# Statistics per pair of heads, another order at the start, and six low-rank products one by one, in a fused attention and MLP kernel

## The chip, the cores and the metric

One core of one Trainium2 chip. The metric is device time in microseconds (us) for one execution, and I quote medians. PE is TensorE, DVE is VectorE, ACT is ScalarE, POOL is GpSimd, SP is SyncE.

## The reference

Cosine attention over 8 batches of 12 heads, 448 tokens and head size 64, then a low-rank token mixer and an MLP. Cut to what matters:

```python
q_n = q / (np.linalg.norm(q, axis=-1, keepdims=True) + 1e-06)
k_n = k / (np.linalg.norm(k, axis=-1, keepdims=True) + 1e-06)
attn = softmax(q_n @ k_n.T / tau)                  # [8, 12, 448, 448]
x = (attn @ v)                                      # heads side by side: [8, 448, 768]
u = x + ((x^T @ U) @ V)^T                           # rank 32 over the tokens
out = u + np.maximum(u @ w_ch1, 0.0) @ w_ch2        # 768 -> 3072 -> 768
```

## The kernel before

Every instruction is an `Op` with an engine, an estimated duration, dependencies, buffers that it takes (`acq`) and gives back (`rel`), and a priority. A planner, `Plan.run`, plays all of them through with the estimated durations, decides each engine's order, and emits them in that order. The program then makes each engine work **strictly in that order** and wait on semaphores. The planner's choice on an engine that isn't PE:

```python
                        for i, (_, _, o) in enumerate(w):
                            if o.start is not None:
                                continue
                            if e == "ACT" and o.fast and free["DVE"] <= t + 1e-9:
                                continue
                            r = self.ready_at(o, e)
                            if r is None:
                                continue
                            if r <= t + 1e-9:
                                pick = o
                                break
                            heapq.heappush(events, r)
                            if r <= t + self.HOLD:
                                break
                        if pick is not None:
                            del w[i]
# ... (cut)
```

The statistics of a group of heads: squares, sums over the 64 elements, then a logarithm and exponential (for the root), an addition, a reciprocal, and the product that normalises q and k:

```python
    def squares(b, g, ld, ops, lo, ii, ss, pr, on, hold):

        red = []
        for i in ii:
            for a0 in range(0, g, G // 2):
                a1 = min(g, a0 + G // 2)
                sq = Slot(r_sq, 1)
                o = Op(on, 0.48 if on == "ACT" else 0.44, None,
                       deps=[ops[i], *hold], acq=[sq], prio=pr + 0.2, fast=True)
                # ... (cut: the square itself, on ACT or DVE)
                red.append(plan.add(Op("DVE", dve_t(256 * (a1 - a0)),
                    lambda i=i, a0=a0, a1=a1, sq=sq: nc.vector.reduce_sum(
                    # ... (cut)
                    deps=[o], acq=[ss], rel=[sq], prio=pr + 0.1)))
        return red
    # ... (cut: scales = squares, then Ln, Exp, addition, reciprocal)
    def stats(b, h0, h1, ld, ops, lo, hold=()):

        pr = 0.3 + 0.03 * h0 if b == 0 else 4
        inv = Slot(r_inv, h1 - h0)
        o, _ = scales(b, h0, h1, ld, ops, lo, (0, 1), inv, pr, "DVE" if b else "ACT/DVE", hold)
        for p in range(h0 // 2, h1 // 2):
            o_ = norm(b, p, ld, lo + 2 * p - h0, inv, 2 * p - h0, {0: o, 1: o}, pr)
        return o_

    def stats_first(ld, ops):

        inv = Slot(r_inv, 3)
        done, ups = {}, []
        for i in range(2):
            done[i], up = scales(0, 0, 2, ld, ops, 0, (i,), inv, -1 - 0.1 * i, ("DVE", "ACT")[i])
            ups.append(up)
        return ups + norm(0, 0, ld, 0, inv, 0, done, -1)
```

In the attention of one pair of heads, seven blocks of scores go to ACT for the exponential and the result lands in one of two `attn` buffers, which the 32 products with v read:

```python
    attn_t = fixed(2, [128, 8, 512], BF, "attn")
    # ... (cut)
        attn = Slot(r_attn, 2)
        # ... (cut: seven scores and exponentials)
                    o = plan.add(Op("PE", 0.033, fn,
                        deps=need + got[b, h, "v"] + attn_set + [v_set[b % 2]] if first else (), acq=[av] if first else [],
                        rel=[attn] if last else []), pe_av)
```

The low-rank products of batch 0, six of them, go as one block in front of the tenth group of up-projections. Each takes one of three PSUM banks `mm`, which the up-projections use too:

```python
    def by_tokens(us, A, X):

        for i in range(3):
            for c0, c1 in ((0, CH), (CH, C)):
                mm = Slot(r_mm, 1)
                o = plan.add(Op("PE", pe_t(CH), lambda i=i, c0=c0, c1=c1, mm=mm: nc.tensor.matmul(
                    out=mm.tile[:, 0:CH], lhsT=V_sb[:, PAD + 128 * i:PAD + 128 * i + 128],
                    rhs=A.tile[:, c0:c1], start=True, stop=True), acq=[mm, us[i]], rel=[A]), pe_mlp)
                # ... (cut: an addition on DVE, which frees the bank)
    # ... (cut)
            if b == 0 and f == 9:
                by_tokens(us, *state["first"])
```

And the order of the start:

```python
    first = lead, [plan.add(Op("SP", 0.45, lambda i=i, src=src: nc.sync.dma_start(
        out=lead.tile[:, i], in_=src[0, 0:2].rearrange("h (s c) d -> s h (c d)", c=SC)),
        acq=[uv], prio=-5, lat=2.5)) for i, src in enumerate((q, k))]
    second = load_qk(0, 2, 4, uses=2)
    ld, ops, _ = load_qk(0, 4, 8)
    id_set = plan.add(Op("POOL", 0.8, lambda: make_identity(nc, ident)), pool_q)
    begun = stats_first(*first[:2])
    stats(0, 2, 4, *second, hold=begun)
    xn_set.append(fill(lambda: nc.vector.memset(xn_t[2][:, 0:8, :], 0.0), 900, prio=0.2, deps=begun))
    zf = fill(lambda: nc.vector.memset(U_f(), 0.0), 400, prio=0.1, acq=[uv], deps=begun)
    u0 = load_u(0)
    v0 = [plan.add(Op("SP", 0.45, lambda t=t: nc.sync.dma_start(out=V_f()[R * t:R * (t + 1)], in_=moe_V),
                      deps=[zf, *begun], prio=-2, lat=12.0)) for t in range(4)]
    u1 = load_u(1)
    stats(0, 4, 8, ld, ops, 0, hold=got[0, 0, "qkT"][2])
    load_v0()
    ld, ops, _ = load_qk(0, 8, 12)
    late = stats(0, 8, 12, ld, ops, 0)
```

## Time and profile before

| | before |
|---|---|
| median of 3 runs | 605.15 us (604.89 to 605.44) |
| span of the profiled run | 603.2 us |
| PE busy / DVE / ACT / POOL | 97% / 50% / 46% / 19% |
| last exponential of batch 0 starts | 37.3 us |
| first unbroken run of up-projections | 41.3 us |

The busy shares say that PE is the bound. They hide the two places where PE is not: the 41 us before the MLP begins, and a hole at 50 us. The prediction below shows the lines for both. For the comparison of stages I use **lost time**: from the trace, the time from the start of one of PE's weight loads to the start of the next, less what the matmul between them needs to stream at full rate (384 columns 0.163 us, 448 columns 0.19 us and so on). It does not depend on the modelled ends of matmuls, nor on some 23 matmul records that are missing from the trace of after.

### The profile page before, as it was taken

The numbers are of one execution on the slowest core, as the hardware profiler recorded it, in microseconds if no ns is written. First come the engines' busy times: TensorE is split into PE (matmuls) and PEld (weight loads), VectorE is DVE, ScalarE is ACT, GpSimd is POOL, SyncE is SP. The second block draws the span as 40 slices with busy tenths as digits, with TensorE's granted clock in tenths as the row PEclk, the third lists the DMA queues.
The fourth block names the chain that finished last, engine by engine and source line by source line (L and its number), as shares of the span: only waits on it lengthen the run. The fifth ranks groups of instructions, "written<-read, shape, count | busy, mean of one in ns | idle before, by whom it ended". The sixth has DMA issues, their size and how long they took to land.

```text
span 603.2 us, 11528 instructions
## 1 busy us (share of the span) xinstructions
PE 586.4 (97%) x4725; PEld 347.0 (58%) x4725; DVE 300.6 (50%) x728; ACT 276.9 (46%) x598; POOL 115.2 (19%) x175
## 2 busy tenths in 40 slices
PE   3899999999999999999999999999999999999997
PEld 1565666555565665666445666566545666654565
DVE  8979749989999988554731244014300210110011
ACT  5877652488874277316741067505642025014300
POOL 8246334062706116000600000000000000000000
PEclk9999999999999999999999999999999999999999
DMA  9999999999999959725922133030002110310021
GB/s 144 193 188 112 204 201 107 150 173 136 159 152 155 149 102 154 95 57 90 123 29 66 52 74 47 1 93 27 15 1 53 52 40 1 90 42 1 0 53 54
DMA packets 150165, 54.81 MB, mean 91 GB/s; under 512 B 115040, under 2 KB 150112, under 8 KB 150112
## 3 DMA queue, kind: packets, MB, share of 16 engines
q0 software_dynamic: 72864, 25.73, 38.4%
q1 hardware_dynamic: 77184, 28.32, 24.4%
q8 instruction: 37, 0.61, 0.4%
q14 instruction: 16, 0.13, 0.1%
q10 hardware_dynamic: 64, 0.02, 0.0%
HBM read 52.25 MB, written 11.01 MB: 105 GB/s over the span
## 4 chain that ended last, share of the span: by engine, by line
PE 93%; DVE 2%; ACT 2%; POOL 1%; DMA 1%; issue 0%; ACTq 0%; POOLq 0%
PE mm L794 36%; PE mm L760 35%; PE sc L572 10%; PE av L592 8%; PE mm L684 1%; PE tp L374 1%; DMA v_nat<-in_v_dram 1%; DVE xn L536 1%; PE mm L649 1%; POOL v_nat L429 1%; ACT attn L577 1%; PE sc L760 0%; POOL qk_nat L396 0%; DVE ss L461 0%; ACT qkT L824 0%
## 5 line engine op out<-in xcount | busy, mean ns | idle before, releaser
L760 PE MATMUL mm<-uT,w_sb 128*128 128x512 bf16 (+1 forms) x1134 | 241.3, 353 | 0.2 <-DVE u_nat L734 0.2
L794 PE MATMUL mm<-w_sb,relu 128*128 128x384 bf16 (+1 forms) x1368 | 231.3, 323 | 0.0
L577 ACT ACTIVATE attn<-sc 128x448 bf16<-128x448 f32 x336 | 164.6, 552 | 110.9 <-PE av L592 58.2
L794 PEld LDWEIGHTS <-relu 128*128 128x128 bf16 x1368 | 132.7, 98 | 86.1 <-issue 0.2
L760 PEld LDWEIGHTS <-w_sb 128*128 128x128 bf16 x1152 | 111.8, 98 | 102.7 <-issue 1.8
L783 ACT ACTIVATE relu<-mm 128x512 bf16<-128x512 f32 (+1 forms) x158 | 86.8, 549 | 129.3 <-PE mm L760 128.7
L803 DVE TENSOR_TENSOR O_sb<-mm,u_nat 128x384 f32<-128x384 f32 (+1 forms) x57 | 31.2, 549 | 210.8 <-PE mm L794 207.4
L572 PE MATMUL sc<-qkT 128*128 128x448 bf16 x336 | 102.7, 356 | 3.7 <-ACT attn L577 2.0
L592 PEld LDWEIGHTS <-attn 128*128 128x128 bf16 x1536 | 62.1, 98 | 17.8 <-issue 2.5
L418 POOL DMA_DIRECT2D v_nat<-in_v_dram x98 | 63.2, 655 | 31.7 <-DMA w_sb<-in_moe_w_ch_dram 15.8
L592 PE MATMUL av<-v_nat,attn 128*128 128x65 bf16 x1536 | 66.6, 194 | 0.8 <-DMA v_nat<-in_v_dram 0.4
L461 DVE TENSOR_REDUCE ss<-sq 112x8 f32<-112x512 bf16 x96 | 63.1, 673 | 0.2
L536 DVE TENSOR_TENSOR xn<-qk_nat,inv 112x512 bf16<-112x512 bf16 x94 | 60.9, 681 | 2.4 <-DMA qkT<-xn 2.2
L396 POOL DMA_DIRECT2D qk_nat<-in_q_dram x24 | 17.2, 718 | 136.5 <-DVE xn L536 117.0
L572 PEld LDWEIGHTS <-qkT 128*128 128x128 bf16 x336 | 28.9, 98 | 22.1 <-issue 7.3
L601 DVE TENSOR_TENSOR X_sb<-av,rd 128x256 bf16<-128x256 f32 x96 | 40.1, 419 | 1.6
L599 DVE RECIPROCAL rd<-av 128x4 f32<-128x4 f32 x96 | 17.1, 179 | 37.6 <-PE av L592 36.9
L457 DVE TENSOR_TENSOR sq<-qk_nat 112x512 bf16<-112x512 bf16 x87 | 33.7, 415 | 0.0
L698 DVE TENSOR_TENSOR u_nat<-mm,X_sb 128x384 bf16<-128x384 f32 x36 | 19.2, 553 | 15.4 <-PE mm L684 15.1
L785 DVE TENSOR_SCALAR relu<-mm 128x384 bf16<-128x384 f32 (+1 forms) x31 | 18.7, 604 | 12.8 <-PE mm L760 12.0
L374 PE MATMUL tp<-ident,xn 112*128 112x112 bf16 x144 | 11.9, 226 | 7.8 <-DVE xn L536 7.6
L474 ACT ACTIVATE ln<-ss 112x32 f32<-112x32 f32 (+2 forms) x26 | 6.0, 231 | 27.3 <-DVE ss L461 27.1
(61 smaller groups left out, 172.5 us busy)
## 6 DMA issues: line engine op xcount, KB each, us to landing
qk_nat<-in_q_dram POOLq DMA_DIRECT2D x23, 224.0 KB, 5.2
qk_nat<-in_k_dram POOLq DMA_DIRECT2D x23, 224.0 KB, 6.3
w_sb<-in_moe_w_ch_dram POOLq DMA_DIRECT2D x4, 1152.0 KB, 14.6
w_sb<-in_moe_w_ch_dram POOLq DMA_DIRECT2D x8, 576.0 KB, 15.8
out_dram<-O_sb SPq DMA_DIRECT2D x15, 168.0 KB, 2.2
out_dram<-O_sb SPq DMA_DIRECT2D x16, 144.0 KB, 2.1
out_dram<-O_sb SPq DMA_DIRECT2D x16, 120.0 KB, 2.0
out_dram<-O_sb SPq DMA_DIRECT2D x16, 96.0 KB, 2.2
```

Source lines behind the costliest of these rows:

```text
L418: nc.gpsimd.dma_start(out=vb[p0:p0 + s1 - s0, hs, j, 0:D], in_=v[b, hs].rearrange("h (s c) d -> c s h d", c=SC)[c, s0:s1]),
L457: nc.vector.tensor_mul(y, x, x)
L461: lambda i=i, a0=a0, a1=a1, sq=sq: nc.vector.reduce_sum(ss.tile[:, i, a0:a1, :].rearrange("p h c -> p (h c)"), sq.tile[:, 0:a1 - a0, :].re ...
L536: nc.vector.tensor_mul(dst, src, sc)
L572: nc.tensor.matmul(out=sc.tile[:, 0:S], lhsT=kT[:, 128 * m:128 * (m + 1)], rhs=qkT.tile[:, 8:12, :].rearrange("p c s -> p (c s)"), start=T ...
L577: exps[m] = plan.add(Op("ACT", act_t(S), lambda sc=sc, m=m: nc.scalar.activation(out=attn.tile[:, m, off:off + S], in_=sc.tile[:, 0:S], fu ...
L592: nc.tensor.matmul(out=av.tile[:, t, 0:D + 1], lhsT=attn.tile[:, m, 128 * t:128 * (t + 1)], rhs=v_t[b % 2][:, h, j, 0:D + 1], start=(j == ...
L601: muls.append(plan.add(Op("DVE", dve_t(256), lambda av=av, rd=rd, h=h: nc.vector.tensor_mul(X.tile[:, :, h * D:(h + 1) * D], av.tile[:, :, ...
L760: o = plan.add(Op("PE", pe_t(n), lambda cc=cc: nc.tensor.matmul(out=mm.tile[:, 0:n], lhsT=w1_sb[:, cc, f * 128:(f + 1) * 128], rhs=uT.tile ...
L783: nc.scalar.activation(out=relu.tile[:, f, 0:n], in_=mm.tile[:, 0:n], func=AF.Relu)
L794: nc.tensor.matmul(out=mm.tile[:, 0:c1 - c0], lhsT=relu.tile[:, f, i * 128:(i + 1) * 128], rhs=w2_t[:, f, c0:c1], start=(f == 0), stop=(f ...
L803: nc.vector.tensor_add(out=O.tile[:, 0:w], in0=mm.tile[:, 0:w], in1=us[i].tile[:, c0:c1]),
```

## The change

Its intent: start the chain of batch 0 earlier and let each pair of heads wait only for its own statistics. (1) ACT makes both of the first squares, and the sums of the second pair come next. (2) The statistics of heads 4 to 8 are split in two groups. (3) The planner is told that v lands later (3.2 us in place of 2.0) and that the products of the first pair with v take longer (0.09 us in place of 0.033), so it puts other work ahead of the products with v. (4) The six low-rank products are spread over six groups of up-projections. The memset of `V_sb` moves from the front to a later place. Cut to its core:

```diff
-                            if e == "ACT" and o.fast and free["DVE"] <= t + 1e-9:
+                            if e == "ACT" and o.fast and "/" in o.eng and free["DVE"] <= t + 1e-9:
-    LATE = 8.0
+    LATE, VLATE = 8.0, 3.2
@@ load_v0
-                n * (0.0055 if hs.step == 2 else 0.011)))
+                n * (0.0055 if hs.step == 2 else 0.011), late=VLATE))
@@ squares: the sums wait for `then` as well
-                    deps=[o], acq=[ss], rel=[sq], prio=pr + 0.1)))
+                    deps=[o, *then], acq=[ss], rel=[sq], prio=pr + 0.1)))
@@ stats_first
-            done[i], up = scales(0, 0, 2, ld, ops, 0, (i,), inv, -1 - 0.1 * i, ("DVE", "ACT")[i])
+            done[i], up = scales(0, 0, 2, ld, ops, 0, (i,), inv, -1 - 0.1 * i, "ACT")
@@ attention: planned length of a product with v of pair 0
-                    o = plan.add(Op("PE", 0.033, fn,
+                    o = plan.add(Op("PE", 0.09 if b == 0 and p == 0 else 0.033, fn,
@@ mlp
-            if b == 0 and f == 9:
-                by_tokens(us, *state["first"])
+            if b == 0 and 9 <= f < 21 and f % 2:
+                by_tokens(us, *state["first"], (f - 9) // 2)
@@ start
-    z = fill(lambda: nc.vector.memset(V_sb, 0.0), 500, prio=-1.3)
+    z = fill(lambda: nc.vector.memset(V_sb, 0.0), 500, prio=3, deps=begun)
-    stats(0, 2, 4, *second, hold=begun)
+    begun_2 = stats(0, 2, 4, *second, hold=begun[:2], then=begun)
-    stats(0, 4, 8, ld, ops, 0, hold=got[0, 0, "qkT"][2])
+    stats(0, 4, 6, *third, hold=last_exp["first"], then=begun_2)
+    stats(0, 6, 8, *third[:2], 2, hold=last_exp["first"], then=begun_2)
 (cut: arguments passed through, two more priorities, a planned landing of q and k,
 the list last_exp["first"], the place of the calls)
```

## The prediction

> **What bounds the kernel now.** I read the page first (span, busy shares, slices), then the busy time by stretches of 5 us, then the rows in order of time of 0 to 40 us, then TensorE alone around 50 us.
>
> ```profile
> span 603.2 us, 11528 instructions
> ...
> PE 586.4 (97%) x4725; PEld 347.0 (58%) x4725; DVE 300.6 (50%) x728; ACT 276.9 (46%) x598; POOL 115.2 (19%) x175
> ```
>
> TensorE is the bound of the whole span, but not of its first 41 us. The chain in order of time shows at 490.6 us the rate at which PE can stream: 144 products of 384 columns in 23.40 us, 0.163 us each, so 0.19 us for 448 columns and 0.032 us for 65. In the first 41 us PE has 42 scores (8.0 us), 192 products with v (6.2 us), 72 transposes at 0.05 us (3.6 us) and some 2.5 us of low-rank products and turned columns: 20 us of work between its first instruction at 7.6 us and the first closed run of up-projections at 41.3 us. Some 13 us are lost there. From 41.3 us on nearly every matmul starts one streaming time after the one before. So the change can earn in only two places: the start, where ACT's exponentials and DVE's statistics set the pace, and one hole at 50 us.
>
> ```profile
> 4.28 0.63 ACT L455 ACTIVATE sq<-raw_uv 112x512 bf16<-112x512 f32 x1 [2.26 <-DMA raw_uv<-in_k_dram]
> 4.34 0.62 DVE L457 TENSOR_TENSOR sq<-raw_uv 112x512 bf16<-112x512 f32 x1
> ...
> 5.00 1.28 DVE L461 TENSOR_REDUCE ss<-sq 112x8 f32<-112x512 bf16 x2
> ...
> 15.39 0.94 PE L374 MATMUL tp<-ident,xn 112*128 112x112 bf16 x8
> ...
> 19.79 0.56 PE L374 MATMUL tp<-ident,xn 112*128 112x112 bf16 x8
> ```
>
> The columns are start, busy us, engine, line, operation, count. The first q square waits on DVE behind eleven memsets; the sums follow it. The same eight transposes take 0.94 us at 15.4 us and 0.56 us at 19.8 us.
>
> ```profile
> 10.62 0.63 ACT L455 ACTIVATE sq<-qk_nat 112x512 bf16<-112x512 bf16 x1 [1.14 <-DVE ss L461]
> 11.16 0.53 ACT L577 ACTIVATE attn<-sc 128x448 bf16<-128x448 f32 x1
> ...
> 14.01 1.01 ACT L577 ACTIVATE attn<-sc 128x448 bf16<-128x448 f32 x2
> 15.81 0.63 ACT L455 ACTIVATE sq<-qk_nat 112x512 bf16<-112x512 bf16 x1 [0.79 <-DVE ss L461]
> ...
> 18.14 1.40 ACT L577 ACTIVATE attn<-sc 128x448 bf16<-128x448 f32 x3
> ...
> 22.94 1.09 ACT L577 ACTIVATE attn<-sc 128x448 bf16<-128x448 f32 x2
> ...
> 26.87 1.03 ACT L824 COPY qkT<-tp 128x672 bf16<-128x672 bf16 x3 [0.43 <-PE tp L374]
> 27.77 8.89 ACT L577 ACTIVATE attn<-sc 128x448 bf16<-128x448 f32 x19
> 36.87 0.98 ACT L577 ACTIVATE attn<-sc 128x448 bf16<-128x448 f32 x2 [0.20 <-PE sc L572]
> ```
>
> Here are the six pairs of heads on ACT, seven exponentials each. Pair 0 begins at 11.16 us though its first scores are out near 10 us: a square stands in front and waits for a buffer. Pairs 1, 2 and 3 begin at 18.1, 22.9 and 27.8 us; then 21 exponentials follow nearly without a break, the last starting at about 37.3 us. The MLP can begin 4 us after that.
>
> ```profile
> 50.01 1.17 PE L730 MATMUL mm<-A_sb,V_sb 128*128 128x384 bf16 x3
> 51.02 0.73 PE L572 MATMUL sc<-qkT 128*128 128x448 bf16 x3
> 51.59 0.56 PE L374 MATMUL tp<-ident,xn 112*128 112x112 bf16 x8
> 52.39 0.79 PE L730 MATMUL mm<-A_sb,V_sb 128*128 128x384 bf16 x2 [0.24 <-DVE u_nat L734]
> ```
>
> This is the hole: from 50.01 to 53.91 us PE starts six of these products (0.98 us), five scores (0.95 us) and eight transposes (0.39 us), 2.3 us of work in 3.9 us. Each product needs one of three PSUM banks, which DVE frees after an addition of 0.55 us that stands behind sums of 0.68 us. 1.6 us are lost.
>
> **What the Trainium skill says.** "Perfetto Trace Analysis", section Identifying the Most-Contended Engine, says that matmul busy time is a poor measure of how near PE is to its limit. The trace agrees: busy time is 4.4 of 5.0 us between 15 and 20 us, where I count only 2.6 us of streaming. "TensorE: Matmul & The Clock Gate", section What's actually happening, gives half rate until about 3.4 us of sustained activity, N/1.2 GHz between starts before and N/2.4 GHz + 2.5 ns after: 93 and 49 ns for 112 columns. The two transpose rows agree ((0.94 - 0.30)/7 = 91 ns, (0.56 - 0.21)/7 = 50 ns). "ScalarE: Activation LUTs", section What ACT_TABLE_LOAD costs, gives 186 ns + 0.833 ns per element and an overlap of 93 ns back to back: 0.47 us from one exponential of 448 to the next. The trace has 0.43 us (four in 1.86 us, the last 0.58 long), and I use that.
>
> **The change part by part.** I followed the new order of the instructions with the old durations, engine by engine. Landings are unchanged, since the POOL queue issues the same transfers in the same order.
>
> First squares. Before, q lands at about 3.6 us (issue at 0.74, 2.9 us to landing) but is squared at 4.34. ACT is idle then and squares it at 3.7 to 4.3, and k at 4.3 to 4.9. DVE loses its square of 0.62 us and a memset of 0.30 us there, so the sums start at about 4.36 in place of 5.00, and everything to the first scores moves by -0.64 us: first transpose 7.62 to 7.0, scores 9.42 to 8.8.
>
> Second pair's sums next, and no square in front of the first exponential. ACT now copies both key blocks; DVE does the two sums at 8.6 to 9.9. Pair 0's exponentials start at 10.0 in place of 11.16. The second pair's scales are ready at about 11.1 in place of 13.4, its transposes at 12.1 in place of 15.4. With 0.9 us of key copies on ACT, pair 1's exponentials start at about 15.4 in place of 18.14: -2.7 us.
>
> Products with v behind their landing. Before, PE stood at the first of them until v landed (0.44 us of wait at 14.3 us), with the second pair's transposes queued behind 17 of them. Now transposes and three scores go first. That is what lets the 15.4 stand; by itself it removes about 1 us of queueing.
>
> Heads 4 to 6 and 6 to 8 apart. It adds one Ln and one Exp on ACT (0.12 us each in the stream) and an addition and a reciprocal on DVE (0.2 and 0.25 us). For that pair 2 waits for two sums of 0.60 us fewer. Pair 2 starts at about 20.2 in place of 22.94 (-2.8), pair 3 at about 24.1 in place of 27.77.
>
> Where this is given back. After three exponentials of pair 3, ACT's next instruction is the q copy of pair 4. Its data need the scales of heads 8 to 12, whose last sum ends at about 23.5; then DVE does two reciprocals and two products for pair 0 first (1.0 us), addition, reciprocal, k and q of pair 4 (2.0 us). The copy is ready at about 26.7, while ACT is free at 25.4: 1.3 us stall. From about 27.2 us 18 exponentials remain, 17 x 0.43 = 7.3 us. Before, this stretch had 1.0 us of stalls for PE; in the new order 44 products with v (two pairs' worth, 1.4 us) stand between scores 3 and 4 of pair 4, with only three PSUM buffers of scores ahead and the bank freed by DVE, so I take 1.8 us. The last exponential starts at 27.2 + 7.3 + 1.8 = 36.3 in place of 37.3. Carried to the MLP: -1.0 us. PE could not follow much further in any case: with a few transposes more in its backlog it has 12 us of work left at 27.2 us.
>
> Low-rank products spread. One of six in front of every second group of up-projections instead of six together. The 1.6 us hole goes, but each still takes one of three banks for 0.16 us of PE work and so shortens the lead of the next group; at six places I charge 0.15 us. Net -0.7 us.
>
> Sum: -1.0 - 0.7 = -1.7 us, with all the rest of the span unchanged. 605.15 - 1.7 = 603.4 us.
>
> **The rivals.** First, the early lead is lost wholly: the 1.3 us stall for pair 4's copy and the products with v in front of its scores. For it: the exponentials run without a break from 27.8 us before, so nothing ahead of that point counts unless pair 4 is earlier too, and I find its scales no earlier than before (25.0 against 25.3). Against it: three exponentials of pair 3 then stand ahead of the copy. It makes 604.4 us.
>
> Second, PE stays cold longer. Before, a run of 30 products with v from 14.3 to 17.5 us stood ahead of the fast rate. Now PE works in pieces until 17 us. Each pair's transposes cost 0.5 us more and each score 0.18 us more while cold; with pair 2 still cold, +0.3 to +0.8 us, so about 604.0 us.
>
> Third, the spread products lose as much as the block did, for the bank rotation is what costs: 604.1 us. If they lose nothing, 602.6 us.
>
> Fourth, the loads of U and V start about 1 us later, since their memset now stands behind the second pair's sums; the casts on POOL and the transfers of batch 1 behind them move by as much. Before, these were issued at 27.9 us, land 5 us later and are first used at 39.7 us; 6 us of slack hide it. Nothing.
>
> **Range and chances.** The two gains can each vanish or double: without both 605.1, with pair 4 on time as well 602.0. The range is 601.8 to 605.1. For 2% the change needs 12 us; all that is lost before 41 us, beyond the 7 us of start, is 13 us, so faster by over 2% has a chance of 0.01, slower 0.01.
>
> **What would show each step.** First transpose near 7.0 us; first exponentials of pairs 0 to 3 near 10.0, 15.4, 20.2, 24.1 us; an ACT wait of about 1.3 us for TensorE before the q copy near 26.7 us; the last exponential of batch 0 near 36.3 us; the first closed run of up-projections near 40.3 us; under 1 us lost around the spread products; everything after that earlier by 1.7 us. I am wrong if pair 3 starts early and the up-projections don't, if transposes near 18 us still take 0.9 us per eight, or if later stages show new idle time of PE.

## The result, and the profile after

604.51 us median of 4 runs (604.14 to 604.91), against 605.3 us (604.89 to 605.69) for the kernel before: ratio 0.9987, 95% interval 0.997 to 1.0004. So **within 2%**, and some 0.8 us faster where 1.7 was predicted. (A ratio is the mean time of one kernel's fast runs over that of the other's of the same rounds, so not quite the ratio of the medians that I quote.) A later repeat of the unedited changed kernel, reported below, gave 0.9987 again, with an interval of 0.9974 to 0.9999.

The span and busy times of the page, after:

```profile
span 602.7 us, 11511 instructions
...
PE 584.3 (97%) x4702; PEld 346.8 (58%) x4725; DVE 300.8 (50%) x729; ACT 278.2 (46%) x601; POOL 114.9 (19%) x175
```

Nothing is to be seen there but 0.5 us less span at the same shares (PE's busy time is 2.1 us less, only in part for some 23 matmul records that are missing from the trace of after: the run with half of the sums, below, misses none and has 584.6 us). The rows in order of time tell more. First the start: ACT of after squares both blocks, and DVE, having nothing else to do, waits for the first.

```profile
3.74 1.33 ACT L455 ACTIVATE sq<-raw_uv 112x512 bf16<-112x512 f32 x2 [1.72 <-DMA raw_uv<-in_q_dram]
...
4.40 1.39 DVE L461 TENSOR_REDUCE ss<-sq 112x8 f32<-112x512 bf16 x2 [0.29 <-ACT sq L455]
```

The sums start at 4.40 in place of 5.00 us, the first transpose at 7.15 in place of 7.62, and the pairs' first exponentials at these times:

| us | pair 0 | pair 1 | pair 2 | pair 3 | pair 4 | pair 5 | last exponential | closed up-projections |
|---|---|---|---|---|---|---|---|---|
| before | 11.17 | 18.15 | 22.95 | 27.78 | 30.76 | 34.37 | 37.32 | 41.29 |
| predicted | 10.0 | 15.4 | 20.2 | 24.1 | | | 36.3 | 40.3 |
| after | 10.13 | 15.35 | 20.48 | 25.02 | 30.46 | 33.87 | 36.97 | 40.94 |

(Times worked out from a trace can differ by 0.01 us from those of its rows.) A lead of 2.5 to 2.8 us for pairs 1, 2 and 3 is down to 0.3 us at pair 4. ACT of after, in order of time, shows where it stands meanwhile:

```profile
25.01 1.42 ACT L577 ACTIVATE attn<-sc 128x448 bf16<-128x448 f32 x3 [0.51 <-PE av L594]
26.95 0.53 ACT L826 COPY qkT<-tp 128x448 bf16<-128x448 bf16 x1 [0.53 <-PE tp L374]
27.38 1.86 ACT L577 ACTIVATE attn<-sc 128x448 bf16<-128x448 f32 x4
30.45 1.42 ACT L577 ACTIVATE attn<-sc 128x448 bf16<-128x448 f32 x3 [1.21 <-PE av L594]
32.15 2.29 ACT L577 ACTIVATE attn<-sc 128x448 bf16<-128x448 f32 x5 [0.29 <-PE sc L572]
```

The brackets give the idle time before the row and what ended it. The copy waits for the transposes of pair 4, as foreseen. The waits on `av`, the PSUM tile of the products with v, at 25.01 and 30.45 I had not foreseen: they are for a **buffer**, as an experiment below shows. Pair 3 writes the `attn` buffer that pair 1 used and pair 4 that of pair 2, and in the new order the products with v that read them come late. Nor did the last statistics come sooner. DVE's last copy of pair 5's q, before and after:

```profile
29.11 0.39 DVE L826 COPY qkT<-tp 128x448 bf16<-128x448 bf16 x1
```

```profile
29.09 0.36 DVE L828 COPY qkT<-tp 128x448 bf16<-128x448 bf16 x1
```

The hole at 50 us is gone. TensorE of after, one of its rows there; the waits for `u_nat` that the prediction shows have no counterpart, and the largest that is left is 0.17 us:

```profile
52.98 0.35 PE L572 MATMUL sc<-qkT 128*128 128x448 bf16 x1 [0.17 <-ACT attn L577]
```

But the busy time by stretches shows that something new stands further on. Columns: stretch, length, then busy us and instructions of PE, PEld, DVE, ACT and POOL, granted clock, DMA share, GB/s. Before, then after:

```profile
50.00:55.00 5.00, 4.22 (x28) 2.17 (x26) 4.96 (x12) 4.19 (x11) 4.44 (x8) 1.00 0.76 49
...
70.00:105.00 35.00, 35.00 (x344) 22.57 (x342) 25.65 (x67) 16.50 (x36) 13.26 (x20) 1.00 1.15 164
```

```profile
50.00:55.00 5.00, 4.71 (x35) 2.82 (x35) 4.89 (x12) 4.09 (x11) 4.42 (x7) 1.00 0.85 54
...
70.00:105.00 35.00, 33.55 (x334) 21.72 (x332) 26.82 (x67) 17.02 (x36) 13.26 (x20) 1.00 1.17 169
```

By these busy times PE was never idle between 70 and 105 us; after the change it is idle for 1.45 us there. All the rows of TensorE in that stretch with an idle time before them, after (before has none):

```profile
76.41 0.75 PE L374 MATMUL tp<-ident,xn 112*128 112x112 bf16 x12 [0.29 <-ACT qkT L826]
86.69 0.59 PE L686 MATMUL sc<-A_sb,V_sb 128*128 128x512 bf16 x2 [0.16 <-issue]
97.98 0.32 PE L796 MATMUL mm<-w_sb,relu 128*128 128x384 bf16 x1 [0.32 <-DVE O_sb L805]
104.55 0.38 PE L374 MATMUL tp<-ident,u_nat 128*128 128x128 bf16 x4 [0.67 <-ACT uT L826]
```

Three of them are waits for PSUM banks that DVE or ACT frees, among work of batch 1 and the MLP of batch 0; for the one of 0.16 us the trace shows no releaser. In lost time:

| stretch, us | before | after | after, repeated |
|---|---|---|---|
| start of the closed up-projections | 41.29 | 40.94 (-0.35) | 41.45 (+0.16) |
| 41.3 to 70 | 2.14 | 1.02 (-1.12) | 0.88 (-1.26) |
| 70 to 105 | 1.21 | 2.74 (+1.53) | 3.02 (+1.81) |
| 105 to 600 | 5.40 | 4.84 (-0.56) | 4.72 (-0.68) |
| sum | | -0.5 | 0.0 |
| span | 603.2 | 602.7 (-0.5) | 603.2 (0.0) |

The sums answer for the spans. So the hole is closed, for more than 1 us, and as much is lost 30 us later in a stage that the diff does not touch.

### The profile page after: what moved, and what is told of

It is laid out like the page before. It is cut to its first block, busy times and chain, and to the rows that moved or that the text cites. A ratio compares the mean times of both kernels' runs of the same rounds, so it can differ in the third digit from the quotient of the medians.

```text
span 602.7 us, 11511 instructions
## 1 busy us (share of the span) xinstructions
PE 584.3 (97%) x4702; PEld 346.8 (58%) x4725; DVE 300.8 (50%) x729; ACT 278.2 (46%) x601; POOL 114.9 (19%) x175
## 4 chain that ended last, share of the span: by engine, by line
PE 92%; DVE 4%; ACT 2%; issue 1%; DMA 0%; ACTq 0%
PE mm L796 36%; PE mm L762 34%; PE sc L572 10%; PE av L594 8%; PE mm L686 1%; DVE xn L536 1%; DVE ss L461 1%; ACT attn L577 1%; PE tp L374 1%; PE mm L651 1%; DVE qkT L828 1%; DMA raw_uv<-in_q_dram 0%; PE sc L762 0%; ACT relu L785 0%; PE sc L686 0%
## 5 line engine op out<-in xcount | busy, mean ns | idle before, releaser
L762 PE MATMUL mm<-uT,w_sb 128*128 128x384 bf16 (+1 forms) x1112 | 236.9, 353 | 1.2 <-ACT relu L785 0.2
L572 PE MATMUL sc<-qkT 128*128 128x448 bf16 x336 | 104.4, 361 | 3.9 <-ACT qkT L826 1.8
L594 PE MATMUL av<-v_nat,attn 128*128 128x65 bf16 x1536 | 65.3, 194 | 0.5 <-DVE X_sb L603 0.5
```

The costliest lines, as they stand in the source:

```text
L572: nc.tensor.matmul(out=sc.tile[:, 0:S], lhsT=kT[:, 128 * m:128 * (m + 1)], rhs=qkT.tile[:, 8:12, :].rearrange("p c s -> p (c s)"), start=T ...
L594: nc.tensor.matmul(out=av.tile[:, t, 0:D + 1], lhsT=attn.tile[:, m, 128 * t:128 * (t + 1)], rhs=v_t[b % 2][:, h, j, 0:D + 1], start=(j == ...
L762: o = plan.add(Op("PE", pe_t(n), lambda cc=cc: nc.tensor.matmul(out=mm.tile[:, 0:n], lhsT=w1_sb[:, cc, f * 128:(f + 1) * 128], rhs=uT.tile ...
```

## The experiments

All twelve were compared with the kernel before on the same chip, the first eight on one, the last four on another; all gave correct results but one. "Up" is the start of the closed run of up-projections in the profiled run (a "first closed relu" in an expectation comes 2.7 us after it). "Full rate" is when TensorE went from half to full rate in that run, by the clock records kept in the trace file; it is 17.77 us in the profile of before and 18.32 us in that of after. What moves it is worked out at the control, below.

| run | median us (runs) | ratio, 95% interval | up, us | full rate, us |
|---|---|---|---|---|
| before + spread only | 604.35 (5) | 0.998, 0.9967 to 0.9992 | 42.16 | 20.63 |
| after, products as one block | 605.38 (5) | 0.9993, 0.9979 to 1.0006 | 41.31 | 19.49 |
| after, third attention buffer | 604.86 (5) | 0.9988, 0.9975 to 1.0 | 41.36 | 19.80 |
| after, v planned as before | 606.0 (5) | 1.001, 0.9998 to 1.0023 | 42.50 | 19.51 |
| after, half of the sums | 603.94 (1) | | 40.45 | 13.36 |
| after, two memsets on POOL | 603.32 (4) | 0.9962, 0.9949 to 0.9976 | 40.05 | 12.54 |
| after, third buffer planned | 604.48 (5) | 0.9981, 0.9968 to 0.9995 | 40.83 | 18.43 |
| after, heads 4 to 8 in one group | 603.9 (5) | 0.9974, 0.9961 to 0.9986 | 40.41 | 18.63 |
| memsets on POOL and one group | 603.91 (5) | 0.9974, 0.9961 to 0.9986 | 40.89 | 17.68 |
| after, first squares as before | 605.04 (5) | 0.9993, 0.998 to 1.0007 | 41.35 | 18.97 |
| memsets on POOL and one group, spread moved by one group | 605.3 (5) | 0.9998, 0.9986 to 1.0011 | 40.77 | 13.20 |
| after again | 604.95 (5) | 0.9987, 0.9974 to 0.9999 | 41.45 | 20.08 |

The kernel before took 605.62 us (9 runs) beside the first four, 605.72 (the same nine and one more) beside the next four, and 605.32 (9) beside the last four.

### The two halves of the change alone

The kernel before with part (4) alone:

```diff
# before
-            if b == 0 and f == 9:
-                by_tokens(us, *state["first"])
+            if b == 0 and 9 <= f < 21 and f % 2:
+                by_tokens(us, *state["first"], (f - 9) // 2)
```

> The kernel before with only the six low-rank products spread over the groups of up-projections. The order of every engine is the same up to 50 us. Theory 1 (two separate gains, the spread one worth about 0.85 us at 50 to 54 us, and part of it given back later because the later order changes): start of the up-projections unchanged at 41.3 us, TensorE loses under 0.8 us between 50 and 54 us in place of 1.6, and the end is 0.3 to 0.9 us earlier than before. Rival (the start alone makes the gain of the whole change): no gain, under 0.2 us.

Measured: 604.35 us, and lost time 0.72 us between 50 and 55 us in place of 1.68. So the spread by itself is a gain. Everything up to 50 us is planned as in the kernel before, and yet its up-projections began at 42.16 us, 0.87 later: the first product with v waited 0.96 us for v to land in this run, 0.44 in the profile of before. TensorE's full rate came later too, at 20.63 us in place of 17.77. That is a first measure of how much the start varies by itself. And there are new waits, one of 0.15 us at 98.89 us and this one:

```profile
105.16 0.38 PE L374 MATMUL tp<-ident,u_nat 128*128 128x128 bf16 x4 [0.65 <-DVE O_sb L803]
```

The changed kernel with part (4) undone:

```diff
# after
-            if b == 0 and 9 <= f < 21 and f % 2:
-                by_tokens(us, *state["first"], (f - 9) // 2)
+            if b == 0 and f == 9:
+                for part in range(6):
+                    by_tokens(us, *state["first"], part)
```

> The changed kernel with the six low-rank products in one block again; all else of the change stays. Theory 1: up-projections start at 40.9 us as in the changed kernel, the hole of about 1.6 us near 50 us is back, and the end is 0.2 to 0.5 us earlier than the kernel before, that is 0.3 to 0.6 us later than the changed kernel. Rival (start alone): as fast as the changed kernel, within 0.15 us.

Measured: 605.38 us, and the whole hole of 1.68 us is back. Its late waits, though the block is back, are those of the run before it (0.15 us at 99.22 us, and this one), where the kernel before has none:

```profile
105.49 0.38 PE L374 MATMUL tp<-ident,u_nat 128*128 128x128 bf16 x4 [0.66 <-DVE O_sb L806]
```

So **either half alone** brings such waits, one of them by touching only the start: they are no property of the spread products. The intervals are too wide to say whether the halves add up.

### Is it the attention buffers that eat the lead?

Pairs 2 and 5 write their exponentials to a third buffer, in space that the second weights use later. First with the same order of instructions:

```diff
# after
-    r_ld, r_xn, r_attn = fixed_ring(ld_t), fixed_ring(xn_t), fixed_ring(attn_t)
+    r_ld, r_xn = fixed_ring(ld_t), fixed_ring(xn_t)
+    r_attn = Ring(2, lambda i: spare_t if i in (2, 5) else attn_t[i - 3] if i in (3, 4) else attn_t[i % 2])
+    spare_t = w2_t.rearrange("p a c -> p (a c)")[:, 0:4096].rearrange("p (b s) -> p b s", b=8)
```

> The changed kernel with the same plan, but pairs 2 and 5 write their exponentials to a third buffer (a part of the not yet loaded second weight), so that pairs 3 and 4 don't reuse a buffer whose products with v are still to come. Theory: the two ACT waits for products with v (0.5 us at 25.0 us, 1.2 us at 30.4 us) are waits for a buffer; both go, the last exponential of the first batch starts 0.6 to 1.2 us earlier than at 37.0 us, and the up-projections start 0.4 to 1.0 us earlier than at 40.9 us. Rival (ACT waits because the scores come late, behind 44 products with v): the wait at 30.4 us stays above 0.8 us and nothing moves. A third: the exponentials move and TensorE, which has no room left, does not: start of the up-projections within 0.2 us.

Measured: both waits on `av` are gone, and nothing is gained (604.86 us; last exponential 37.39). The wait has moved to the scores, which stand behind 44 products with v in PE's order, as the prediction feared. ACT of this run:

```profile
27.78 3.17 ACT L579 ACTIVATE attn<-sc 128x448 bf16<-128x448 f32 x7
32.57 1.85 ACT L579 ACTIVATE attn<-sc 128x448 bf16<-128x448 f32 x4 [1.62 <-PE sc L574]
```

Then with the planner knowing of the third buffer, so that it can place scores and products with v anew:

```diff
# the run before it
-    r_attn = Ring(2, lambda i: spare_t if i in (2, 5) else attn_t[i - 3] if i in (3, 4) else attn_t[i % 2])
+class Ring3(Ring):
+    def free_at(self, k=0):
+        i = self.n + k
+        old = i - 3 if i < 8 else i - 2
+        return 0.0 if old < 0 else self.freed.get(old)
+    r_attn = Ring3(2, lambda i: spare_t if i in (2, 5) else attn_t[i - 3] if i in (3, 4) else attn_t[i % 2])
```

> The third buffer again, but now the plan counts with it and places scores and products with v anew. Theory (the second half of the wait for pair 4 was the place of its scores behind 44 products with v): the ACT waits of 1.2 us for products with v and of 1.6 us for scores near 30 to 32.5 us are both under 0.6 us, the last exponential is at 36.4 us or earlier (37.0 in the changed kernel). Rival (TensorE and VectorE have no room): 36.7 us or later.

Measured: the exponentials run almost without a break and the last starts at 34.60 us, 2.4 us earlier than in after.

```profile
29.04 3.32 ACT L587 ACTIVATE attn<-sc 128x448 bf16<-128x448 f32 x7
32.05 3.36 ACT L587 ACTIVATE w_sb<-sc 128x448 bf16<-128x448 f32 x7
36.02 0.59 ACT L836 CAST A_sb<-mm 128x512 bf16<-128x512 f32 x1 [0.62 <-PE mm L661]
```

The up-projections begin at 40.83 us, 0.1 earlier, and the time is 604.48 us. With 2.4 us less on ACT there is nothing to gain in this order: PE still has its products with v, low-rank products and turned columns to do, and in the third line ACT waits for it. In this run the exponentials are **not** the bound: the up-projections begin 6.24 us after the last of them, where in all the other thirteen profiles it is 3.98 or 3.99 us. That isn't a limit at 37 us, for three runs below end their exponentials at 36.07 to 36.46 us and begin the up-projections as much earlier. From 32 us to the up-projections PE loses only 0.5 to 0.95 us in these thirteen, so what sets their start is mainly what PE has lost before 32 us.

### Which parts of the start count?

The products with v planned as in the kernel before:

```diff
# after
-    LATE, VLATE = 8.0, 3.2
+    LATE, VLATE = 8.0, 2.0
-                    o = plan.add(Op("PE", 0.09 if b == 0 and p == 0 else 0.033, fn,
+                    o = plan.add(Op("PE", 0.033, fn,
```

> The changed kernel with the two planning constants of the products with v set back (landing 2.0 in place of 3.2, 0.033 in place of 0.09 for the first pair). Its order puts all 32 products with v of pair 0 ahead of the scores of pair 1, behind the second pair's transposes. Theory (VectorE's sum of work sets when pair 4 can be scored, so early pairs have slack): pair 1's exponentials start 1.5 us or more later, near 17 us, but the scales of heads 8 to 12 move by less than 0.5 us and the up-projections start within 0.4 us of the changed kernel. Rival (each pair's start counts to the end): up-projections 1 us or more later, end at or above the kernel before.

Measured: 606.0 us, the last exponential at 38.53 in place of 36.97. ACT's longest wait in it is again for scores behind products with v that stand waiting:

```profile
17.15 1.42 ACT L577 ACTIVATE attn<-sc 128x448 bf16<-128x448 f32 x3 [1.75 <-PE sc L572]
```

So part (3) is what keeps the start from being a loss: up-projections at 42.50 us are 1.6 us later than in the first profile of after and 1.05 later than in its repeat, and the ratios (1.001 against 0.9987) differ by 1.4 us, though their intervals overlap a little. I had thought the early pairs had slack enough to hide it; they have not.

The first q square back on DVE:

```diff
# after
-            done[i], up = scales(0, 0, 2, ld, ops, 0, (i,), inv, -1 - 0.1 * i, "ACT")
+            done[i], up = scales(0, 0, 2, ld, ops, 0, (i,), inv, -1 - 0.1 * i, ("DVE", "ACT")[i])
```

> The changed kernel with the first q square back on DVE, the only edit. My theory: the start of the first transpose goes from 7.15 back to about 7.7 us, but the early pairs' lead was not what set the first up-projections, so the first closed relu moves by less than 0.3 us and the time stays within 0.2 us of the changed kernel. The rival, that what the first transpose gains is carried to the end, has relu at 44.2 us and a time of +0.6 us.

Measured: 605.04 us, against 604.95 for the unedited kernel in the same job: nothing. The sums start at 4.69 us, between after's 4.40 and before's 5.00. So of the 0.60 us that the sums had moved, half comes from the squares, and the other half, as I read it, from the memset of 0.30 us that went from in front of them; at the first transpose (7.32 against 7.15 and 7.22 in the two profiles of after) 0.1 us to 0.2 us is left of it, and none at the up-projections (41.35 against 40.94 and 41.45). My expectation of 7.7 us for the transpose was wrong, having given the squares what the memset did.

The statistics of heads 4 to 8 in one group again:

```diff
# after
-    stats(0, 4, 6, *third, hold=last_exp["first"], then=begun_2)
-    stats(0, 6, 8, *third[:2], 2, hold=last_exp["first"], then=begun_2)
+    stats(0, 4, 8, *third, hold=last_exp["first"], then=begun_2)
```

> The changed kernel with heads 4 to 8 in one group of statistics again; the rest of the change stays. Theory (the split only lets pair 2 start earlier and costs VectorE 0.4 us): pair 2's exponentials start 0.8 us or more later than at 20.5 us, pair 4's not later than 0.4 us, the up-projections within 0.4 us of 40.9 us, the end within 0.4 us of the changed kernel. Rival (the split is a main part of the gain): up-projections 0.8 us later or more.

Measured: pairs 2 and 3 start at 22.25 and 26.72 us, 1.7 us later than in after, and the end is *earlier*: pair 4 at 29.78 (30.46 in after), last exponential at 36.44, up-projections at 40.41, and 603.9 us. Its median is 0.6 and 1.0 us under the two medians of after. So what gave the change its name gains nothing and probably costs, about half a microsecond in the profile (full rate at 18.63 us, near the 18.32 of after): pairs 2 and 3 come early to a queue that is set by pair 4, and, as I read it, the extra instructions on DVE and ACT delay pair 4. The medians are of different jobs and their intervals overlap, so a cost is not settled.

### Is it VectorE's work?

The sums of batch 0 over 32 of the 64 elements (a **wrong result on purpose**, one look):

```diff
# after
-                        sq.tile[:, 0:a1 - a0, :].rearrange("p h (c d) -> p (h c) d", d=D),
+                        sq.tile[:, 0:a1 - a0, :].rearrange("p h (c d) -> p (h c) d", d=D)[
+                            :, :, 0:D // 2 if b == 0 and on == "ACT/DVE" else D],
```

> A wrong result on purpose: in the changed kernel the ten sums of squares of heads 2 to 12 read half of their elements (about 0.27 us less each, 2.7 us of VectorE in all); plan and order stay. Theory (VectorE's work between 9 and 29.5 us sets when the last pairs can be scored, whatever the order): the last key or query copy of the first batch ends 1.5 to 2.5 us earlier than 29.45 us, pair 4's query copy on ACT starts 1 to 2 us earlier than 26.95 us, the last exponential 0.8 us or more earlier than 36.97 us. Rival (the exponentials and TensorE's products with v set it): the last exponential moves by less than 0.4 us though VectorE is done earlier.

Measured: about 2.7 us less work for DVE, and its last copy of batch 0 starts 0.49 us earlier (28.60 in place of 29.09), the last exponential 0.49 us and the up-projections 0.49 us. A bound by the sum of DVE's work would have moved by 2.7. Even the 0.49 need not come from the sums, for TensorE was at full rate from 13.36 us in this run. What sets the pace is, as I read the waits, the chain that goes from DVE to ACT to PE and back in a fixed order, each waiting for one of the others in turn.

The memsets of `xn[2]` and `V_sb` given to POOL, behind its loads of the first weights:

```diff
# after
-    xn_set.append(fill(lambda: nc.vector.memset(xn_t[2][:, 0:8, :], 0.0), 900, prio=0.41, deps=begun))
-    z = fill(lambda: nc.vector.memset(V_sb, 0.0), 500, prio=3, deps=begun)
+    xn_set.append(Op("POOL", 0.6, lambda: nc.gpsimd.memset(xn_t[2][:, 0:8, :].bitcast(mybir.dt.uint32), 0)))
+    z = Op("POOL", 0.4, lambda: nc.gpsimd.memset(V_sb.bitcast(mybir.dt.uint32), 0))
+    for o in (xn_set[2], z):
+        plan.add(o, pool_q)        # after the two loads of the first weights
```

> The changed kernel with two memsets (0.48 us of the third normalized tile, 0.30 us of V) moved from VectorE to GpSimd, behind the issues of the first weight's loads, where it waits for data; the plan makes its order anew. Theory: 0.78 us less on VectorE between 8 and 11 us; pairs 1 to 4 begin 0.3 to 0.8 us earlier, the up-projections 0.3 to 0.7 us earlier than at 40.9 us. The end: 0.3 to 0.7 us earlier than the changed kernel unless the new order loses it between 70 and 105 us. Rival: no change of the start beyond 0.2 us.

Measured: 603.32 us, **the fastest of all**, 2.4 us under the kernel before of its job, up-projections at 40.05 us. It takes 0.78 us of work off DVE (memsets of 0.48 and 0.30 us) and has the up-projections 0.9 to 1.4 us earlier than the two profiles of after. There is a second thing in it. TensorE runs at half rate at first, and in this run it reached the full rate at 12.5 us, where after reached it at 18.3 us, and its repeat at 20.1. The score in this line takes 0.35 us; one at half rate takes 0.56:

```profile
12.68 0.35 PE L572 MATMUL sc<-qkT 128*128 128x448 bf16 x1
```

I can't separate the two gains; the four runs lie within 0.3 us of each other.

Both improvements together:

```diff
# the run with the memsets on POOL
-    stats(0, 4, 6, *third, hold=last_exp["first"], then=begun_2)
-    stats(0, 6, 8, *third[:2], 2, hold=last_exp["first"], then=begun_2)
+    stats(0, 4, 8, *third, hold=last_exp["first"], then=begun_2)
```

> The changed kernel with two edits that each were faster alone: the two memsets of 1152 and 448 columns on the idle POOL (603.3 us, 0.9962 of the kernel before), and the statistics of heads 4 to 8 in one group again (603.9 us, 0.9974). If both shorten the same in-order chain from VectorE's statistics to TensorE's backlog, the gains add: the first closed relu at about 42.2 us (42.75 and 43.11 alone) and 602.8 us, ratio 0.9953. If TensorE's own backlog is the bound by then, as the run with three attention buffers suggested, relu stays at 42.7 and the time at 603.3.

Measured: 603.91 us, which neither of the two expectations had: the gains do not add, and the sum is no better than the single group alone. DVE is now so early that squares of q of heads 8 to 12 stand in its order before their q has landed, and everything behind them waits too, the addition, reciprocal and products for heads 4 to 8 first of all: pair 2 starts at 23.07 us. DVE, TensorE, and the busy time by stretches of this run:

```profile
16.77 0.76 DVE L457 TENSOR_TENSOR sq<-qk_nat 112x512 bf16<-112x512 bf16 x2 [1.21 <-DMA qk_nat<-in_q_dram]
```

```profile
19.99 0.97 PE L374 MATMUL tp<-ident,xn 112*128 112x112 bf16 x12 [1.62 <-DVE xn L536]
21.19 1.30 PE L374 MATMUL tp<-ident,xn 112*128 112x112 bf16 x12 [0.23 <-DVE xn L536]
```

```profile
20.00:25.00 5.00, 4.65 (x44) 2.83 (x45) 4.93 (x14) 3.87 (x12) 0.98 (x1) 0.66 1.27 221
```

PE stands for 1.62 us. The twelve transposes after that are still at full rate, 49 ns from start to start; their 0.97 us has a wait of 0.2 us in it. The next twelve start 93 ns apart and take 1.30 us, where twelve at full rate take 0.76 (the run with the memsets on POOL has such a row at 19.99 us). So PE has fallen back to half rate between the two rows, by the clock records at 21.09 us and for 3.41 us, and the granted clock of the stretch is 0.66. Four of the five runs have a mean clock of 0.996 or 0.997, as such a stretch makes it, and took 603.68 to 604.57 us; the one at 1.0 took 603.11. The slowest run of the kernel before in this job, 606.43 us, has 0.997 too. The run of 603.11 us is the best single time here, but five runs are what counts, and the version of choice is the one with the memsets on POOL alone.

### Do the late waits belong to the spread?

The same kernel, with the six products one group of up-projections later:

```diff
# the run with both improvements
-            if b == 0 and 9 <= f < 21 and f % 2:
-                by_tokens(us, *state["first"], (f - 9) // 2)
+            if b == 0 and 10 <= f < 22 and f % 2 == 0:
+                by_tokens(us, *state["first"], (f - 10) // 2)
```

> As the run with POOL memsets and one group of statistics, with the six low-rank products of batch 0 in front of the even groups of up-projections 10 to 20 in place of the odd ones 9 to 19. If the stalls of TensorE of 0.7 to 0.8 us near 97 and 103 us belong to spreading as such, they are there with the same sizes. If they are an accident of where the planned order of batch 1's work falls, their sizes and places change: between 70 and 105 us the lost time of 2.3 to 2.7 us becomes anything from 1.2 (as in the kernel before) to 3; the time moves by the same. I lean to the second.

Measured: 605.3 us, 1.4 us slower for nothing but another place of six products. The waits have other places and sizes. With the odd groups only two small ones were left, though the products are spread there as in after:

```profile
77.12 0.48 PE L762 MATMUL mm<-uT,w_sb 128*128 128x384 bf16 x2 [0.24 <-ACT qkT L826]
88.19 0.59 PE L686 MATMUL sc<-A_sb,V_sb 128*128 128x512 bf16 x2 [0.16 <-issue]
```

With the even groups there are these, and again one of 0.16 us:

```profile
78.01 0.83 PE L796 MATMUL mm<-w_sb,relu 128*128 128x384 bf16 x4 [0.45 <-DVE relu L787]
...
94.96 1.46 PE L796 MATMUL mm<-w_sb,relu 128*128 128x384 bf16 x8 [0.67 <-DVE O_sb L805]
112.52 0.23 PE L374 MATMUL tp<-ident,u_nat 128*128 128x128 bf16 x1 [0.78 <-DVE u_nat L700]
```

Lost time is 2.1 us between 70 and 105 us, where the run with the odd groups has 1.7, and 1.3 us between 105 and 115, where that one has none. So these waits are an accident of where the planned order of batch 1's attention falls against the MLP of batch 0. It is the order and not the moment: the waits of 0.32 and 0.67 us that after has at 98 and 104.6 us stand in nine of the profiles, whose up-projections begin anywhere from 40.05 to 42.50 us. The kernel before had, at this place, an order with no such wait.

### The control

The changed kernel, unedited, once more:

> The changed kernel itself, unedited, in the same job as the other three: a control for what a profile and a median vary by. 604.5 us (0.4 either way), ratio 0.9987; first closed relu 43.6 us within 0.5; stalls of TensorE near 76, 97 and 104 us as in its first profile.

Measured: 604.95 us, ratio 0.9987, as the first time. From 65 us on its waits are those of the first profile. But its up-projections began at 41.45 us, not 40.94. The same instructions in the same order parted at the transposes of pair 2. TensorE in the first profile of after, then in the control:

```profile
18.41 0.56 PE L374 MATMUL tp<-ident,xn 112*128 112x112 bf16 x8
```

```profile
18.55 0.94 PE L374 MATMUL tp<-ident,xn 112*128 112x112 bf16 x8
```

In one the full rate has come by 18.4 us, in the other, by the spacing of the matmul starts, only at 20.1. Pair 2's first exponential is 0.5 us later (20.99 against 20.48), and the 0.5 us stays to the up-projections. It has the size that the second rival of the prediction gave ("+0.3 to +0.8"), but it comes in some runs only, and with the old order too: there full rate came at 17.77 us in one profile and at 20.63 in the other. So it isn't shown to be an effect of the change.

The clock records tell when it comes. They change on a grid of steps of 3.41 us (17.68, 21.09 and 24.51 us in the run with both improvements), which lies differently in every run. I cut all fourteen traces into such steps and added up the streaming time of PE in each, at the rate in force and with the transposes. A step at half rate was followed by full rate where it held 2.68 us or more (16 steps), and never where it held 2.67 or less; a step at full rate was followed by half rate in the two that held 0.74 and 1.08 us, and never where it held 1.31 or more. That holds in these traces; so here work in pieces delayed the full rate, and how the grid lay was chance.

The five runs of the control fall in two groups, 603.97 and 604.12 us, and 604.95 to 605.08; I take the groups to be such states of the grid. The mean clocks support it: they are 0.999 in the two fast runs and in the first profile of after, 1.0 in the three slow ones, the profiled one among them. (After PE's last product the clock falls to half again, at 602.00 us in the first profile, which is inside its span, and at 603.75 us in the control, which is after its end.) But only one of the five has a trace.

## Why the prediction was right or wrong

The time stayed within 2% and, at 604.5 us, inside the range, whose centre was 1.1 us too low. That is partly luck: the range reached up to 605.1 us, so to almost no gain at all, and the sum is made of other terms than the prediction's. All three signs of being wrong that it named are there: pair 3 is 2.2 to 2.8 us early and the up-projections gain 0.35 us at most, eight transposes near 18 us still take 0.94 us in the repeat, and PE has new idle time later. By its steps:

- **What bounds the kernel, and where it can gain**: right as to the start and the hole. "From 41.3 us on nearly every matmul starts one streaming time after the one before" was right of the kernel before and carried over to the kernel after without reason.
- **First squares**: sums at 4.36 predicted, 4.40 found; first transpose 7.0 predicted, 7.15 and 7.22 found. But half of this is probably the memset's doing, and the run with the squares undone shows that nothing is left at the up-projections. (Before, twelve memsets stood on DVE ahead of the square, not eleven.)
- **Pairs 0 to 3**: 10.0, 15.4, 20.2 and 24.1 predicted; 10.13, 15.35, 20.48 and 25.02 found (10.19, 15.42, 20.99 and 25.55 in the repeat). Right for the first two. Pair 2 is later by 0.5 us in the repeat, where PE is still at half rate; pair 3 also by 0.51 us for an `attn` buffer, a wait that the prediction did not have.
- **Products with v**: the prediction let the order stand and put about 1 us on it; undone alone it costs 1.05 to 1.6 us. Right.
- **Heads 4 to 6 and 6 to 8 apart**: predicted as a lead of 2.8 us for pair 2, and 2.5 us is there (2.0 in the repeat), at the cost of four small instructions. What seems to have failed is the tacit step that this costs nothing at pair 4: the run with one group has pair 4 earlier by 0.7 us.
- **Where this is given back**: 1.3 us of stall for pair 4's copy were predicted and 0.53 found, with another 0.51 for pair 3's buffer ahead of it (with the third buffer, where that wait is gone, the copy waits 1.15 us); exponentials resume at 27.38 (27.2 predicted). From there 1.8 us of stalls were predicted, and 1.21 + 0.29 + 0.26 = 1.76 found, though the largest is for a buffer and not for scores. Yet the last exponential is at 36.97 and not 36.3. The missing 0.5 us is what the sum left out: after each wait the exponentials lose their overlap. From 27.38 to 36.97 are 9.59 us; 17 steps of 0.43 and 1.76 of waits make 9.07.
- **Carried to the MLP, -1.0 us**: this term failed. -0.35 us in the first profile, +0.16 in the repeat. The kernel before varies here as well (41.29 us, and 42.16 in the run with its start), so by two profiles of the old start and three of the new (40.94, 41.31, 41.45) the mean gain is 0.5 us, with a scatter as large. The planned third buffer shows that the exponentials alone do not give more: 2.4 us off them gave 0.1 us at the up-projections. More was to be had where PE lost less before 32 us, as in the run with the memsets on POOL (40.05 us).
- **Low-rank products, -0.7 us**: too small where they stand. The lost time from 41.3 to 70 us fell by 1.12 and 1.26 us; six places were charged 0.15 us each, and in sum some 0.5 us was lost.
- **"With all the rest of the span unchanged"**: this step failed, and it is the one that decides. +1.53 us (1.81) of new waits of PE between 70 and 105 us, -0.56 (-0.68) beyond. The prediction names "new idle time of PE" in later stages as a sign that it is wrong; the sign is there. With the planner an edit at 10 us re-orders what follows at 100 us, as the two halves alone and the spread moved by one group show.
- **What it read in the skill and the trace**: of the 4.4 us of busy time between 15 and 20 us it counts only 2.6 as streaming, but PE was at half rate until 17.77 us; at the rate in force it is 3.8 us. The two rates of a matmul, N/1.2 GHz and N/2.4 GHz + 2.5 ns, stand one section further on in that page, under "Wait — 56ns, not 53.3ns?".

The first rival, the lead wholly lost at 604.4 us, came nearest to the time and was about right of the start. It has the right number with the wrong remainder, for it too left the rest of the span unchanged.

What stays open: how much of the gain with memsets on POOL comes from the earlier full rate of PE; whether the split costs, and how much; and why the medians give 0.8 us where the two profiles of after against the one of before give 0.5 and 0.0. The profiled run of before, at 604.94 us, was among its fast ones (its runs go from 604.6 to 606.4), so at least part of that is which run was profiled, and how the clock's grid lay in it.

## What to carry to other kernels

Where a planner or a scheduler fixes each engine's order, a local gain must be checked against the whole span: compare the idle time of the bounding engine stage by stage, for the new order may lose elsewhere what it won. Before giving early work a lead, find the instruction at which the queue closes again (here pair 4's copy, then PE's backlog), for only what moves that one counts. And an order that is tight against a landing turns, when everything ahead gets faster, into an engine that stands still with ready work behind it.

## What the Trainium skill lacked or had wrong

- "TensorE: Matmul & The Clock Gate", section What's actually happening, says that the moment of full rate varies by 500 ns either way from run to run. In two runs of the kernel after it came at 18.32 and 20.08 us, in two with the order of before at 17.77 and 20.63, and with slightly other orders from 12.5 us on. Where PE works in pieces, the spread is larger than the page says, and in after it is worth 0.5 us of the start.
- The same section gives one idle window of some 3.4 us for the fall back to half rate. The length of the step agrees (3.41 us between clock records), but it need not be idle: steps with 1.08 and 0.74 us of streaming were enough. The first has the wait of 1.62 us in it. Waits of 0.90 us at full rate (two in the run with the memsets on POOL) had no such effect.
- "Perfetto Trace Analysis", section Optimization Strategy, says to take the regimes of a kernel apart and find the gaps of the engine in each. The runs agree (PE 97% before and after, with 1.45 us of idle time new in one stretch). What it lacks is that closing a gap in one stage can open one in another, where one order is planned for all: six products moved by one group of up-projections made +1.4 us.
- "ScalarE: Activation LUTs", section What ACT_TABLE_LOAD costs, has figures from which one works out 0.47 us, as an estimate, from one 448-element exponential to the next; the traces have 0.43 us in a stream, and some 0.5 us in sum for four breaks in it.
- No page has it that the granted clock in the views does not tell the first half-rate stretch, beyond a general warning that clock records are not to be relied on: it stands at 1.00 from 5 to 20 us in the control, where eight transposes take 0.94 us, because the records of that trace begin with the change to full rate at 20.08 us. From there on they agree with the spacing of the matmul starts.
